# Moving a residual's transposes from TensorE to DMA, re-laying the last tokens' phases, and a new step order in a one-core attention and mixing kernel

## The chip, the core and the metric

The kernel runs on one core of one Trainium2 chip. The metric is the device time of one execution in microseconds (us). Runs more than 1.5% above the kernel's fastest count as slow and are left out of ratios. A ratio in this text is the mean time of one kernel's fast runs over the mean of the other's fast runs of the same rounds, so it is not quite the ratio of the medians that stand beside it. The 95% interval goes with it.

## The reference, cut to what matters

Inputs are q, k, v of 8 batches x 8 heads x 576 tokens x 64. The first half is attention twice: on tokens averaged by four (144 of them), repeated back, plus a band of seven tokens around each token. Its output becomes x, 576 tokens x 512 channels per batch. The second half is:

```python
theta = x @ w_theta
zr, zi = x * np.cos(theta), x * np.sin(theta)
y = w_tok_r @ zr + w_tok_i @ zi        # over tokens, per batch
u = x + y
return u + np.maximum(u @ w_ch, 0.0)
```

## The kernel before

One generator per step of a batch; a string of letters gives the order in which the steps are emitted, and every engine keeps exactly that order. L loads, C casts on POOL, A turns q and k, S scores, N and V attention outputs, T makes x transposed (channels on partitions), H phases, Z modulation, X mix, R channels, O output. PSUM has two wide slots and four of one bank each, taken in rotation.

Phases and modulation work on 128 tokens at a time; the last 64 tokens stand twice on the partitions, once for cosine and once for sine:

```python
for c in range(5):                                   # H
    n = OC[c]                                        # 128, 128, 128, 128, 64
    for dc in range(4):
        for lo in range(0, P, n):                    # twice for the last 64
            nc.tensor.matmul(out=th[lo:lo + n, :], lhsT=xT[:, dc, P*c:P*c + n], rhs=wth[:, dc, :], ...)
    # ... sine and cosine on ACT
for c in range(5):                                   # Z
    # ... nc.tensor.transpose of xT into psxt, then DVE: z = psxt * (cos, sin)
```

The mix yields u transposed (`uT`); the channel step multiplies it by `w_ch` and also turns it back on TensorE for the residual:

```python
nc.tensor.matmul(out=psr, lhsT=uT[:, dc, P*c:P*c + P], rhs=wch[:, dc, :], ...)      # R, four of these
nc.tensor.transpose(out=psx[:, P*dc:P*dc + P], in_=uT[:, dc, P*c:P*c + P], identity=ident)   # and four
nc.scalar.activation(out=rel, in_=psr, func=AF.Relu)
nc.vector.tensor_tensor(out=osb, in0=rel, in1=psx, op=ALU.add)                      # O, then the store
```

The softmax here doesn't subtract the row's maximum and nothing guards it: scores larger than these inputs give would overflow.

## Time and profile before

| | before |
|---|---|
| time, runs seen with the prediction | 277.8 us (274.64 to 278.04) |
| profiled span | 272.3 us |
| first mix matmul | 55.3 us |
| last matmul | 266.7 us |
| TensorE idle between the two | 0.1 us |

### The profile page before, as it was taken

The page shows a single profiled execution, that of the slowest core. Times are in us where ns is not written, and L with a number is a line of the kernel's source. Part 1 is how long each engine was busy: PE and PEld are TensorE (multiplying, and loading weights), DVE is VectorE, ACT ScalarE, POOL GpSimd, SP SyncE. Part 2 cuts the span into 40 slices and gives each one's busy share as a digit, 9 for nine tenths or more (in the row PEclk, how much of TensorE's full clock was granted, in tenths as well). Part 3 has the DMA queues.
Part 4 walks back from the last instruction along what each step waited for, and adds up shares of the span by engine and source line. Part 5 has one row for each costly group of instructions (what it writes and reads, how often), then busy time and mean ns, then how long its engine had stood idle before and what let it go on. Part 6 is the DMA issues. An engine that isn't in the chain of part 4 may idle for free.

```text
span 272.3 us, 7503 instructions
## 1 busy us (share of the span) xinstructions
PE 250.1 (92%) x2965; PEld 175.7 (65%) x2992; DVE 188.4 (69%) x423; ACT 183.3 (67%) x338; POOL 159.2 (58%) x187
## 2 busy tenths in 40 slices
PE   0486988999999999999999999999999999999991
PEld 0344654688558865787568865877668766766761
DVE  4958798778664885578656875667887676765542
ACT  2644279655887778877987789769887976543031
POOL 4236855999839974597729790998956526200000
PEclk9999599999999999999999999999999999999999
DMA  7999999999889895899449962984491002201223
GB/s 199 247 237 287 258 218 216 211 202 262 144 193 235 197 206 132 175 204 204 130 115 226 209 166 56 197 211 130 138 217 30 19 2 79 79 22 39 87 89 135
DMA packets 107858, 43.57 MB, mean 160 GB/s; under 512 B 97456, under 2 KB 101552, under 8 KB 107824
## 3 DMA queue, kind: packets, MB, share of 16 engines
q1 hardware_dynamic: 107824, 43.10, 71.2%
q8 instruction: 23, 0.38, 0.6%
q14 instruction: 11, 0.09, 0.1%
HBM read 33.65 MB, written 9.44 MB: 158 GB/s over the span
## 4 chain that ended last, share of the span: by engine, by line
PE 78%; DMA 11%; POOL 3%; DVE 2%; ACT 2%; issue 1%; SPq 0%; DVEq 0%; POOLq 0%
PE psu L583 26%; PE psth L541 11%; PE psr L602 10%; PE pstr L322 6%; DMA st_v<-in_v_dram 5%; PE psxt L562 4%; PE psS L414 4%; PE psloc L491 4%; DMA stw_th<-in_moe_w_theta_dram 4%; PE xTps L521 3%; PE psx L607 2%; DMA stw_tok<-in_moe_w_tok_i_dram 2%; PE psnd L453 2%; PE psr L615 1%; PE wps L262 1%
## 5 line engine op out<-in xcount | busy, mean ns | idle before, releaser
L583 PE MATMUL psu<-WT,z 128*128 128x288 bf16 x576 | 79.7, 286 | 0.0
L583 PEld LDWEIGHTS <-z 128*128 128x128 bf16 x576 | 53.3, 98 | 13.3
L435 POOL TENSOR_SCALAR_AFFINE_SELECT pm<-pm 128x1024 bf16<-128x1024 bf16 (+1 forms) x35 | 36.7, 1050 | 38.5 <-ACT pm L422 38.4
L587 DVE TENSOR_TENSOR uT<-psu,xT 128x288 bf16<-128x288 f32 x64 | 29.2, 457 | 25.9 <-PE psu L583 25.2
L422 ACT ACTIVATE pm<-psS 128x1024 bf16<-128x1024 f32 (+1 forms) x40 | 38.5, 983 | 11.6 <-PE psS L414 11.4
L541 PE MATMUL psth<-wth,xT 128*128 128x512 bf16 (+1 forms) x181 | 39.9, 381 | 0.8
L437 POOL TENSOR_SCALAR_AFFINE_SELECT pm<-pm 128x1024 bf16<-128x1024 bf16 (+1 forms) x35 | 36.8, 1051 | 2.4
L636 DVE TENSOR_TENSOR osb<-rel,psx 128x512 f32<-128x512 f32 (+1 forms) x40 | 25.2, 632 | 18.7 <-ACT rel L627 13.7
L627 ACT ACTIVATE rel<-psr 128x512 f32<-128x512 f32 (+1 forms) x40 | 22.2, 556 | 22.6 <-PE psr L602 15.3
L602 PE MATMUL psr<-wch,uT 128*128 128x512 bf16 x114 | 32.2, 380 | 0.7
L564 DVE TENSOR_TENSOR z<-psxt,cs 128x1024 bf16<-128x1024 bf16 (+1 forms) x40 | 24.6, 632 | 9.5 <-PE psxt L562 6.9
L500 DVE TENSOR_TENSOR tmp<-psloc,rl 120x512 bf16<-120x512 f32 (+1 forms) x40 | 27.6, 690 | 1.4
L547 ACT ACTIVATE cs<-psth,pihc 128x512 bf16<-128x512 f32 x32 | 22.1, 689 | 8.6 <-PE psth L541 7.9
L139 POOL CAST v_w<-st_v 128x1024 bf16<-128x1024 f32 (+1 forms) x24 | 21.0, 899 | 10.9 <-DMA st_v<-in_v_dram 10.9
L522 DVE TENSOR_TENSOR xT<-xTps,xdT 128x480 bf16<-128x480 bf16 (+1 forms) x40 | 24.8, 631 | 2.7 <-PE xTps L521 2.5
L325 ACT CAST kT<-pstr 128x384 bf16<-128x384 f32 x36 | 17.5, 485 | 8.3 <-PE pstr L322 8.1
L541 PEld LDWEIGHTS <-xT 128*128 128x128 bf16 (+1 forms) x192 | 14.0, 101 | 13.1 <-issue 3.3
L325 ACT CAST qT<-pstr 128x384 bf16<-128x384 f32 x36 | 16.2, 483 | 9.1 <-PE pstr L322 8.9
L133 POOL CAST k_tm<-st_k 96x1024 bf16<-96x1024 f32 x18 | 18.5, 1037 | 4.7 <-DMA st_k<-in_k_dram 4.7
L548 ACT ACTIVATE cs<-psth 128x512 bf16<-128x512 f32 x32 | 19.0, 592 | 0.0
L491 PE MATMUL psloc<-v_w,pm 128*128 128x65 bf16 (+1 forms) x320 | 17.0, 197 | 2.1 <-DVE xd L466 1.8
L133 POOL CAST q_tm<-st_q 96x1024 bf16<-96x1024 f32 x18 | 18.3, 1037 | 0.0
(98 smaller groups left out, 423.0 us busy)
## 6 DMA issues: line engine op xcount, KB each, us to landing
st_v<-in_v_dram SPq DMA_DIRECT2D x32, 256.0 KB, 5.4
out_dram<-osb SPq DMA_DIRECT2D x32, 256.0 KB, 2.4
st_q<-in_q_dram SPq DMA_DIRECT2D x36, 192.0 KB, 4.5
st_k<-in_k_dram SPq DMA_DIRECT2D x36, 192.0 KB, 4.6
st_q<-in_q_dram SPq DMA_DIRECT2D x8, 288.0 KB, 5.7
st_k<-in_k_dram SPq DMA_DIRECT2D x8, 288.0 KB, 5.3
st_v<-in_v_dram SPq DMA_DIRECT2D x8, 200.0 KB
stw_tok<-in_moe_w_tok_r_dram SPq DMA_DIRECT2D x4, 288.0 KB, 4.8
```

The source lines that it names most:

```text
L133: eng[i](out=dst[:, 2 * c:2 * c + 2].rearrange("p c h d -> p (c h d)"), in_=staged.pop((b, f"{'qk'[i]}{c}"))[0:TR])
L325: nc.scalar.copy(out=To[:, :, TR * c:TR * c + TR], in_=ps[:, :, 0:TR])
L422: nc.scalar.activation(out=pv, in_=ps[0:kw].rearrange("p e (j w) -> p (e j) w", w=P)[:, :, 0:qn], func=AF.Exp, scale=SCL,)
L435: nc.gpsimd.affine_select(out=pv, in_=pv, compare_op=ALU.is_ge, fill=0.0, base=off, pattern=[[0, 8], [-1, qn]], channel_multiplier=1)
L437: nc.gpsimd.affine_select(out=pv, in_=pv, compare_op=ALU.is_ge, fill=0.0, base=6 - off, pattern=[[0, 8], [1, qn]], channel_multiplier=-1)
L491: nc.tensor.matmul(out=pv[0:qn, par, j, :], lhsT=pms[b][c][0:kw, 4 * par + j, 0:qn], rhs=v_w[0:kw, c, 2 * j + par, 0:65], start=(j == 0), ...
L500: nc.vector.tensor_tensor(out=tmp[0:cnt].rearrange("p (j e d) -> p e j d", e=2, j=4), in0=pv[0:cnt, :, :, 0:D], in1=rl[0:cnt].unsqueeze(3) ...
L541: nc.tensor.matmul(out=th[lo:lo + n, :], lhsT=xT[:, dc, P * c:P * c + n], rhs=wth[:, dc, :], start=(dc == 0), stop=(dc == 3),)
L583: nc.tensor.matmul(out=ps[:, 0:288], lhsT=z[:, j, P * dc:P * dc + P], rhs=WT[:, j, cols], start=(j == 0), stop=(j == 8),)
L587: nc.vector.tensor_tensor(out=uT[:, dc, cols], in0=ps[:, 0:288], in1=xT[:, dc, cols], op=ALU.add)
L602: nc.tensor.matmul(out=psr, lhsT=uT[:, dc, P * c:P * c + P], rhs=wch[:, dc, :], start=(dc == 0), stop=(dc == 3),)
L636: nc.vector.tensor_tensor(out=osb[:, 0:w], in0=rel[:, 0:w], in1=psx[:, 0:w], op=ALU.add)
```

## The change

Its intent: take work from TensorE, the bound.

1. Residual: `uT` is turned by DMA transposes (SBUF to SBUF) issued by SyncE, and one DVE operation does relu and addition.

```diff
-nc.tensor.transpose(out=psx[...], in_=uT[:, dc, P*c:P*c + P], identity=ident)
-nc.scalar.activation(out=rel, in_=psr, func=AF.Relu)
-nc.vector.tensor_tensor(out=osb, in0=rel, in1=psx, op=ALU.add)
+# in the mix, as soon as a chunk of 128 channels is complete
+nc.sync.dma_start_transpose(out=ur[:, :, P*dc:P*dc + P], in_=uT[:, dc, 0:512])
+nc.gpsimd.tensor_copy(out=ut[:, dc % 2, HALF*(dc // 2):...], in_=uT[:, dc, 512:576])
+if dc >= 2: nc.sync.dma_start_transpose(out=utr[:, dc - 2, :].unsqueeze(1), in_=ut[:, dc - 2, :])
+# in the output
+nc.vector.scalar_tensor_tensor(out=osb, in0=psr, scalar=0.0, in1=ur[:, c, :], op0=ALU.max, op1=ALU.add)
```

2. Phases of the last 64 tokens: computed with channels on partitions, multiplied there, and turned by one DMA transpose. Their modulation step disappears.

```diff
+for ec in range(4):
+    for dc in range(4):
+        nc.tensor.matmul(out=th[:, ec, :], lhsT=wth[:, dc, P*ec:P*ec + P], rhs=xT[:, dc, 512:576], ...)
+# ... two sines of 256, zT = xT * (cos, sin)
+nc.sync.dma_start_transpose(out=z[:, 8, :].rearrange(...), in_=zT.rearrange(...))
```

3. q and k of batches 0 and 1 are loaded as nine tokens a partition on 128 partitions (before: six on 96), and the casts of batch 0 move from DVE and ACT to ACT and POOL. 4. A new order string for the whole program, and four output tiles for two.

More of the change, by code (lines that the diff above doesn't have):

```diff
@@ L35 @@
 WIDE = 2
+WR = 9
+WP = S // WR
 TR = 96
-NTR = 6
 TP = TR // 4
@@ L92, in load @@
                     nc.sync.dma_start(
-                        out=stage(b, f"{nm}{hh}")[0:TR, 0:2 * NTR * D].rearrange("p (h e) -> p h e", h=2),
-                        in_=src[b, 2 * hh:2 * hh + 2].rearrange("h (p r) d -> p h (r d)", r=NTR),
+                        out=stage(b, f"{nm}{hh}")[:, 0:WR * D],
+                        in_=src[b, 2 * hh:2 * hh + 2].rearrange("h (p r) d -> (h p) (r d)", r=WR),
                     )
@@ L116, in cast @@
     def cast(b):
-        q_tm = work.tile([TR, NTR, H, D], BF16, tag="q_tm", bufs=1, name=f"q_tm{b}")
-        k_tm = work.tile([TR, NTR, H, D], BF16, tag="k_tm", bufs=1, name=f"k_tm{b}")
+        dims = [P, 2, WR, 2, D] if b < WIDE else [P, 6, H, D]
+        q_tm = work.tile(dims, BF16, tag="q_tm", bufs=1, name=f"q_tm{b}")
+        k_tm = work.tile(dims, BF16, tag="k_tm", bufs=1, name=f"k_tm{b}")
         v_w = v_ws[b % 2]
@@ L125, in cast @@
                 for i, dst in enumerate((q_tm, k_tm)):
-                    eng[i](out=dst[:, :, 2 * hh:2 * hh + 2, :].rearrange("p r h d -> p h r d"),
-                           in_=staged.pop((b, f"{'qk'[i]}{hh}"))[0:TR, 0:2 * NTR * D].rearrange(
-                               "p (h r d) -> p h r d", h=2, d=D))
+                    eng[i](out=dst[:, hh // 2, :, hh % 2, :],
+                           in_=staged.pop((b, f"{'qk'[i]}{hh}"))[:, 0:WR * D].rearrange("p (r d) -> p r d", d=D))
                     yield
@@ L132, in cast @@
                 for c in range(3):
-                    eng[i](out=dst[:, 2 * c:2 * c + 2].rearrange("p c h d -> p (c h d)"),
+                    eng[i](out=dst[0:TR, 2 * c:2 * c + 2].rearrange("p c h d -> p (c h d)"),
                            in_=staged.pop((b, f"{'qk'[i]}{c}"))[0:TR])
@@ L158 @@
     nc.vector.tensor_copy(out=ip[:, 0:TR], in_=ident[0:TR, 0:TR])
-    pihc = const.tile([P, 2], FP32, name="pihc")
+    pihc = const.tile([P, 1], FP32, name="pihc")
     nc.vector.memset(pihc, PIH)
-    nc.vector.memset(pihc[HALF:P, 1:2], 0.0)
     kdPs = []
@@ L216 @@
     dve, act, gp = nc.vector.tensor_copy, nc.scalar.copy, nc.gpsimd.tensor_copy
-    CASTS = {0: (dve, act, gp), None: (gp, gp, gp)}
+    CASTS = {0: (act, gp, gp), None: (gp, gp, gp)}
     wth = wpool.tile([P, 4, DM], BF16, name="wth")
@@ L292, in turns, with wide_turn @@
         parts[b] = (qT, kT, qdT, kdP)
-        def wide_turn(n, hh):
+        def wide_turn(n, i):
             tm, To = ((q_tm, qT), (k_tm, kT))[n]
-            ps = w2(f"pstr{n}{hh}_{b}")
-            for r in range(NTR):
-                nc.tensor.matmul(
-                    out=ps[:, r // 3, (r % 3) * TR:(r % 3) * TR + TR],
-                    lhsT=tm[:, r, 2 * hh:2 * hh + 2, :], rhs=ip[:, 0:TR], start=True, stop=True,
-                )
-            (dve if n == 1 else act)(
-                out=To[:, hh, :].rearrange("p (w k c) -> p w k c", k=2, c=3),
-                in_=ps[:, :, 0:3 * TR].rearrange("p k (c w) -> p w k c", w=TR),
-            )
+            pss = [w2(f"pstr{n}{2 * i + a}_{b}") for a in range(2)]
+            for r in range(WR):
+                for a in range(2):
+                    nc.tensor.matmul(
+                        out=pss[a].rearrange("p k e -> p (k e)")[:, WP * r:WP * r + WP],
+                        lhsT=tm[WP * a:WP * a + WP, i, r, :, :], rhs=ident[WP * a:WP * a + WP, WP * a:WP * a + WP],
+                        start=True, stop=True,
+                    )
+            for a in range(2):
+                hh = 2 * i + a
+                (dve if n == 1 and a == 1 else act)(
+                    out=To[:, hh, :].rearrange("p (w r) -> p w r", r=WR),
+                    in_=pss[a].rearrange("p k e -> p (k e)")[:, 0:S].rearrange("p (r w) -> p w r", w=WP),
+                )
@@ L307, in wide_turn @@
             with nc.allow_low_precision(reason="sums are taken in float32 and rounded once"):
+                hs = slice(2 * i, 2 * i + 2)
                 if n == 0:
-                    nc.vector.tensor_reduce(out=qdT[:, hh, :], in_=To[:, hh, :].rearrange("p (m j) -> p m j", j=4),
-                           axis=AX.X, op=ALU.add)
-                else:
-                    nc.vector.tensor_reduce(out=kdP[:, hh, 0:4, 0:30],
-                       in_=To[:, hh, 0:480].rearrange("p (g m j) -> p g m j", g=4, j=4),
-                           axis=AX.X, op=ALU.add)
-                    nc.vector.tensor_reduce(out=kdP[:, hh, 4, 0:24], in_=To[:, hh, 480:576].rearrange("p (m j) -> p m j", j=4),
-                           axis=AX.X, op=ALU.add)
+                    nc.vector.tensor_reduce(out=qdT[:, hs, :], in_=To[:, hs, :].rearrange("p e (m j) -> p e m j", j=4),
+                                            axis=AX.X, op=ALU.add)
+                else:
+                    for hh in range(2 * i, 2 * i + 2):
+                        nc.vector.tensor_reduce(out=kdP[:, hh, 0:4, 0:30],
+                                                in_=To[:, hh, 0:480].rearrange("p (g m j) -> p g m j", g=4, j=4),
+                                                axis=AX.X, op=ALU.add)
+                    nc.vector.tensor_reduce(out=kdP[:, hs, 4, 0:24],
+                                            in_=To[:, hs, 480:576].rearrange("p e (m j) -> p e m j", j=4),
+                                            axis=AX.X, op=ALU.add)
@@ L322, in turn @@
                 nc.tensor.matmul(
-                    out=ps[:, hh, :], lhsT=tm[:, c, 2 * hh:2 * hh + 2, :], rhs=ip, start=True, stop=True,
+                    out=ps[:, hh, :], lhsT=tm[0:TR, c, 2 * hh:2 * hh + 2, :], rhs=ip, start=True, stop=True,
                 )
@@ L334, in turn @@
                                    in_=ps[:, :, TR + lo - TP * c:TR + hi - TP * c])
-        for i in range(8 if b < WIDE else 12):
+        for i in range(4 if b < WIDE else 12):
             if b < WIDE:
@@ L363, with slot @@
     pds, pms, xds, tmps = {}, {}, {}, {}
+    def slot(b, h):
+        return (2 * (h // 4) + h % 2, h // 2 % 2) if b < WIDE else (h // 2, h % 2)
     def scores(b):
@@ L394, in scores @@
         for h in range(H):
-            par, r = h % 2, KP * (h % 4)
+            r = KP * (h % 4)
+            blk, par = slot(b, h)
             nc.tensor.matmul(
                 out=ps[r:r + KP, h // 4, SD:2 * SD],
-                lhsT=kdP[64 * par:64 * par + 64, h // 2, 4, :],
-                rhs=qdT[64 * par:64 * par + 64, h // 2, :],
+                lhsT=kdP[64 * par:64 * par + 64, blk, 4, :],
+                rhs=qdT[64 * par:64 * par + 64, blk, :],
                 start=True, stop=True,
@@ L452, in pooled_out @@
             for h in range(H):
+                blk, par = slot(b, h)
                 nc.tensor.matmul(
                     out=pv[:, h // 4, h % 4, :],
-                    lhsT=pd[:, h, QD * g:QD * g + QD], rhs=vd[:, 0, h, 0:65],
+                    lhsT=pd[:, 2 * blk + par, QD * g:QD * g + QD], rhs=vd[:, 0, h, 0:65],
                     start=(h % 4 == 0), stop=False,
@@ L488, in outputs @@
             pv = ps[:, :, 0:260].rearrange("p e (j w) -> p e j w", w=65)
-            for par in range(2):
-                for j in range(4):
-                    nc.tensor.matmul(
-                        out=pv[0:qn, par, j, :],
-                        lhsT=pms[b][c][0:kw, 4 * par + j, 0:qn],
-                        rhs=v_w[0:kw, c, 2 * j + par, 0:65],
-                        start=(j == 0), stop=(j == 3),
-                    )
+            for h in range(H):
+                blk, par = slot(b, h)
+                nc.tensor.matmul(
+                    out=pv[0:qn, h // 4, h % 4, :],
+                    lhsT=pms[b][c][0:kw, 4 * par + blk, 0:qn],
+                    rhs=v_w[0:kw, c, h, 0:65],
+                    start=(h % 4 == 0), stop=(h % 4 == 3),
+                )
             rl = work.tile([P, 2, 4], FP32, tag="rl", name=f"rl{c}_{b}")
@@ L500, in outputs @@
             nc.vector.tensor_tensor(
-                out=tmp[0:cnt].rearrange("p (j e d) -> p e j d", e=2, j=4),
+                out=tmp[0:cnt].rearrange("p (e j d) -> p e j d", e=2, j=4),
                 in0=pv[0:cnt, :, :, 0:D],
@@ L535, in phases @@
         xT = xTs[b]
-        for c in range(5):
+        z = zs[b] = moep.tile([P, 9, DM], BF16, tag="z", name=f"z{b}")
+        for c in range(4):
             th = w1(f"psth{c}_{b}")
-            n = OC[c]
             for dc in range(4):
-                for lo in range(0, P, n):
-                    nc.tensor.matmul(
-                        out=th[lo:lo + n, :], lhsT=xT[:, dc, P * c:P * c + n], rhs=wth[:, dc, :],
-                        start=(dc == 0), stop=(dc == 3),
-                    )
-            cs = css[b, c] = moep.tile([P, 2, DM], BF16, tag="cs", bufs=3, name=f"cs{c}_{b}")
-            if c < 4:
-                nc.scalar.activation(out=cs[:, 0, :], in_=th, func=AF.Sin, bias=pihc[:, 0:1], scale=1.0)
-                nc.scalar.activation(out=cs[:, 1, :], in_=th, func=AF.Sin, bias=0.0, scale=1.0)
-            else:
-                nc.scalar.activation(out=cs[:, 0, :], in_=th, func=AF.Sin, bias=pihc[:, 1:2], scale=1.0)
-            yield
+                nc.tensor.matmul(
+                    out=th, lhsT=xT[:, dc, P * c:P * c + P], rhs=wth[:, dc, :],
+                    start=(dc == 0), stop=(dc == 3),
+                )
+            cs = css[b, c] = moep.tile([P, 2, DM], BF16, tag="cs", bufs=3, name=f"cs{c}_{b}")
+            nc.scalar.activation(out=cs[:, 0, :], in_=th, func=AF.Sin, bias=pihc, scale=1.0)
+            nc.scalar.activation(out=cs[:, 1, :], in_=th, func=AF.Sin, bias=0.0, scale=1.0)
+            yield
@@ new lines, in phases @@
+        th = w1(f"pstt_{b}")[:, 0:4 * HALF].rearrange("p (e t) -> p e t", e=4)
+        for ec in range(4):
+            for dc in range(4):
+                nc.tensor.matmul(
+                    out=th[:, ec, :], lhsT=wth[:, dc, P * ec:P * ec + P], rhs=xT[:, dc, 512:576],
+                    start=(dc == 0), stop=(dc == 3),
+                )
+        cst = moep.tile([P, 4, 2, HALF], BF16, tag="cst", bufs=1, name=f"cst_{b}")
+        nc.scalar.activation(out=cst[:, :, 0, :], in_=th, func=AF.Sin, bias=pihc, scale=1.0)
@@ L553, in modulate @@
+        nc.scalar.activation(out=cst[:, :, 1, :], in_=th, func=AF.Sin, bias=0.0, scale=1.0)
+        zT = moep.tile([P, 4, 2, HALF], BF16, tag="zT", bufs=1, name=f"zT_{b}")
+        nc.vector.tensor_tensor(
+            out=zT, in0=xT[:, :, 512:576].unsqueeze(2).to_broadcast([P, 4, 2, HALF]), in1=cst, op=ALU.mult,
+        )
+        nc.sync.dma_start_transpose(
+            out=z[:, 8, :].rearrange("p (e d) -> p e d", e=4), in_=zT.rearrange("p e r t -> p (e r t)"),
+        )
+        yield
     def modulate(b):
-        xT = xTs[b]
@@ L556, in modulate @@
-        z = zs[b] = moep.tile([P, 9, DM], BF16, tag="z", name=f"z{b}")
-        for c in range(5):
+        xT, z = xTs[b], zs[b]
+        for c in range(4):
             ps = w1(f"psxt{c}_{b}", BF16)[:, 0:DM]
-            n = OC[c]
             for dc in range(4):
-                for lo in range(0, P, n):
-                    nc.tensor.transpose(out=ps[lo:lo + n, P * dc:P * dc + P], in_=xT[:, dc, P * c:P * c + n], identity=ident)
-            m = 2 if c < 4 else 1
+                nc.tensor.transpose(out=ps[:, P * dc:P * dc + P], in_=xT[:, dc, P * c:P * c + P], identity=ident)
@@ L564, in modulate @@
             nc.vector.tensor_tensor(
-                out=z[:, 2 * c:2 * c + m, :], in0=ps.unsqueeze(1).to_broadcast([P, m, DM]),
-                in1=css.pop((b, c))[:, 0:m, :],
-                op=ALU.mult,
+                out=z[:, 2 * c:2 * c + 2, :], in0=ps.unsqueeze(1).to_broadcast([P, 2, DM]),
+                in1=css.pop((b, c)), op=ALU.mult,
             )
             yield
-    uTs = {}
+    uTs, urs = {}, {}
     def mix(b):
@@ L577, in mix @@
         uT = uTs[b] = moep.tile([P, 4, S], BF16, tag="uT", name=f"uT{b}")
+        ur = moep.tile([P, 4, DM], BF16, tag="ur", name=f"ur{b}")
+        ut = moep.tile([P, 2, P], BF16, tag="ut", bufs=1, name=f"ut{b}")
+        utr = moep.tile([P, 2, P], BF16, tag="utr", name=f"utr{b}")
+        urs[b] = ur, utr
         for dc in range(4):
@@ L587, in mix @@
                 nc.vector.tensor_tensor(out=uT[:, dc, cols], in0=ps[:, 0:288], in1=xT[:, dc, cols], op=ALU.add)
+                if hf == 1:
+                    nc.sync.dma_start_transpose(out=ur[:, :, P * dc:P * dc + P], in_=uT[:, dc, 0:512])
+                    nc.gpsimd.tensor_copy(out=ut[:, dc % 2, HALF * (dc // 2):HALF * (dc // 2) + HALF], in_=uT[:, dc, 512:576])
+                    if dc >= 2:
+                        nc.sync.dma_start_transpose(out=utr[:, dc - 2, :].unsqueeze(1), in_=ut[:, dc - 2, :])
                 yield
@@ L596, in channels @@
         for c in range(5):
-            psr = w1(f"psr{c}_{b}")
-            psx = w1(f"psx{c}_{b}", BF16)
+            psr = rels[b, c] = w1(f"psr{c}_{b}")
             if c < 4:
-                w = DM
                 for dc in range(4):
@@ L605, in channels @@
                     )
-                for dc in range(4):
-                    nc.tensor.transpose(
-                        out=psx[:, P * dc:P * dc + P], in_=uT[:, dc, P * c:P * c + P], identity=ident,
-                    )
             else:
-                w = DM // 2
                 for dc in range(4):
@@ L615, in channels @@
                         nc.tensor.matmul(
-                            out=psr[64 * hf:64 * hf + 64, 0:w], lhsT=uT[:, dc, 512:576],
-                            rhs=wch[:, dc, w * hf:w * hf + w],
+                            out=psr[64 * hf:64 * hf + 64, 0:256], lhsT=uT[:, dc, 512:576],
+                            rhs=wch[:, dc, 256 * hf:256 * hf + 256],
                             start=(dc == 0), stop=(dc == 3),
                         )
-                for j in range(2):
-                    for hf in range(2):
-                        nc.tensor.transpose(
-                            out=psx[64 * hf:64 * hf + 64, P * j:P * j + P],
-                            in_=uT[:, 2 * hf + j, 512:576], identity=ident,
-                        )
-            rel = moep.tile([P, DM], FP32, tag="rel", name=f"rel{c}_{b}")
-            nc.scalar.activation(out=rel[:, 0:w], in_=psr[:, 0:w], func=AF.Relu)
-            rels[b, c] = (rel, psx, w)
             yield
     def store(b):
+        ur, utr = urs.pop(b)
         for c in range(5):
-            rel, psx, w = rels.pop((b, c))
-            osb = moep.tile([P, DM], FP32, tag="osb", name=f"osb{c}_{b}")
-            nc.vector.tensor_tensor(out=osb[:, 0:w], in0=rel[:, 0:w], in1=psx[:, 0:w], op=ALU.add)
+            psr = rels.pop((b, c))
+            w = DM if c < 4 else DM // 2
+            osb = moep.tile([P, DM], FP32, tag="osb", bufs=4, name=f"osb{c}_{b}")
+            nc.vector.scalar_tensor_tensor(
+                out=osb[:, 0:w], in0=psr[:, 0:w], scalar=0.0,
+                in1=ur[:, c, :] if c < 4 else utr.rearrange("p j d -> p (j d)"), op0=ALU.max, op1=ALU.add,
+            )
             if c < 4:
@@ L642, in store @@
             yield
-    FIRST = (
-        "LCLACLLCAALCCLALLCALCACLAASCLDSCLSCSLAlDVSLNNLcVVCLlNClcATDALTSClCADTCSlVccLlllCcLcCCHlVLTcclHTCLcLA"
-        "ZlcZClLAHAAHHLLDCSAccAWLCZSLSWCCWWSWWCCLWSCLWWSZZLNASAAlXLVClXAXLAVAAXcANAXNTVAXcATLXSCVTAHCVXTHLTZH"
-        "CRHOCZLCHLZSZZRROCOSXARLCLLROLLO"
-    )
-    PERIOD = (
-        "SSXAXAANCAXAASCNAXACNLVLAXCLAVVALAXTSSCTTRROCOVACHLVXTHTZHZHHZROCSZLLZRCLLOSRXO"
-    )
-    PERIODS = 3
-    LAST = (
-        "LASLNAAXAACSXCALANAACCVXCAXSSCNXVAAXCAVAAROSSTTRSOCSXTAALVRSROTSVHONLTHVLZNHZLHZHZZACVCASNXXTAVAXAAC"
-        "LCVXAVARCTSSOXATSSTXTHNXVHZZHNVHHNZSXZRZORSSOXTTVRROVHOXXXTROVXTXZTHHZHXXZZHZRORROXOXXRXOXXXROROXROR"
-        "ROORO"
+    ORDER = (
+        "LLLCCCLCLLDLlLALCLlALCClLACCClALcScSSlCSSCAcVlLclCCSDVNNlcVLcLcDLCCVLNTTSlclTCALlHVLCTCcZLCLHAlDTLAH"
+        "cCAHLCcLLHcSWCWZLAWCLSSZWAWNSCWLWWCCSZAWALLNXLSACVNXTAASXVAAAXXLACTVLXlClAVXVAXCSCSTLTACSDAATSHNcHNZ"
+        "HNCcVHZVLHLCTZSLZCARSOTRLOCACARSLLALAOCXAROVXCAAXVAROALHVTCXSSXXCATASSZXALTCHHXVNHNAHAVCSNALRLLSLLCT"
+        "LORROOCAAZLSZZATCVRCOXALXALXTXAVVXCLASCXSASTSACXTHNHVNZHAVCCHZXACNROATAHTLSZZSRLORLOLRSRLHLOOCLVAXXC"
+        "ACVATAAVXTATCHHZXHXAZCHALLCSCZXSXAZSSXLNCARLASLLCONXAAVSXNVXCLSCAAAXATVRAOXVRAOAXTSRCTCSORSVOXACLSTS"
+        "RTHNOXNAVZHVZCHLHNHLLRSZLCRLLLRCOOCOTCZRSAOXAAXATXAAAVVXAAXCTATAVCCSXSTSROXASSHXVHNNHZHNZVHTZSRORTSO"
+        "ZROVXHTVXXTVHZHXTXZHZHXZROXRXOXXXXROXXROXXRORORRRORROOROOO"
     )
@@ L685 @@
     pin()
-    for s in FIRST + PERIOD * PERIODS + LAST:
+    for s in ORDER:
         next(sequences[s])
```

## The prediction

> **What bounds the kernel now.** I read the page first (busy shares, slices), then the chain that ended last in order of time, then four windows cut at the landmarks of that chain, then the groups by form, the DMA issues, and SyncE's own waits. The windows carry most of the argument. Columns: length, then busy us and instructions of PE, PEld, DVE, ACT and POOL, the granted clock, the DMA engines' mean busy share, GB/s.
>
> ```profile
> 0.00:47.00 47.00, 31.93 (x324) 19.27 (x328) 36.15 (x96) 25.02 (x36) 24.54 (x45) 0.93 1.05 238
> 47.00:55.50 8.50, 8.30 (x139) 5.96 (x137) 6.64 (x16) 5.67 (x9) 7.89 (x10) 1.00 1.24 210
> 55.50:204.00 148.50, 147.56 (x1848) 106.22 (x1862) 104.59 (x232) 118.22 (x234) 110.95 (x116) 1.00 0.83 179
> 204.00:272.30 68.30, 62.35 (x661) 44.30 (x666) 40.97 (x82) 34.36 (x63) 15.84 (x17) 1.00 0.18 59
> ```
>
> Three stages. To 47 us the DMA engines are full (share 1.05 at 238 GB/s) and PE isn't. From 55.5 us, where the first mix matmul of batch 0 stands, PE is busy 147.6 of 148.5 us, and it stays so to its last matmul at 266.7. The third stage is a tail of 5.6 us. The chain shows what ends the first stage, the start of the second, and the tail:
>
> ```profile
> 17.92 9.70 DMA stw_th<-in_moe_w_theta_dram
> 33.48 7.37 DMA st_v<-in_v_dram
> 41.09 6.39 DMA stw_tok<-in_moe_w_tok_i_dram
> 47.54 1.29 POOL wtm L248 x2
> 48.87 1.12 PE wps L262 x11
> ...
> 55.47 1.10 PE psu L583 x9
> ...
> 265.46 0.70 DVE osb L636
> 266.18 2.00 DMA out_dram<-osb
> 268.30 0.42 DVE osb L636
> ```
>
> The start waits for the last token weight (landed 47.5), is then cast and turned by PE, and only then can a mix run. At the end the chain runs PE, relu, addition, store; the last addition waits for a store to free one of only two output tiles.
>
> **What PE pays for the parts that go.** These pieces of the chain, in order of time, are PE's issue spacing, which is what counts where PE never idles (the busy column overlaps matmuls and overstates it):
>
> ```profile
> 56.57 0.24 PE psloc L491 x8
> ...
> 137.09 0.22 PE psx L607 x4
> ...
> 139.91 0.56 PE psr L615 x8
> 140.47 0.11 PE psx L622 x4
> ...
> 246.50 0.98 PE psth L541 x8
> 247.48 0.22 PE psxt L562 x8
> ```
>
> Four 128x128 transposes of the residual cost 0.22 us, the last 64 tokens' four 0.11. The eight phase matmuls of those tokens cost 0.98, not eight times the 0.215 of a full 512-column one: their two halves of the array run together. Their eight transposes cost 0.22. The first row is there for its shape: eight matmuls of 65 columns on 128 rows of weights take 0.24.
>
> **What the Trainium skill says.** (1) "DMA: Bandwidth & Descriptors", section "Latency and other measured facts": an X-bar transpose ran at 261 GB/s with a non-contiguous middle dimension. No DMA transpose is in this trace, so this is the size I use, and it is the weakest number here. (2) Same page, "Anatomy of one DMA": about 2.0 us fixed, mostly the write's receipt. That is for another issuing path, but this trace agrees: with the DMA engines nearly idle after 204 us, a 64 KB store landed in 1.9 us and a 256 KB one in 2.0. (3) Same page, "Queues, rings and completion order": each DMA engine takes descriptors in ring order, so a transpose issued by SyncE stands behind the loads issued before it. The trace agrees in so far as stores landed in 4.2 us at 111 to 141 us, beside loads, against 2.0 without them. (4) "VectorE: DVE Perf Modes", "The perf-mode tier table": an operand in PSUM with fp32 keeps an element-wise operation at the slow rate. The trace agrees: additions and products reading a 512-wide fp32 tile take 0.69 us. So the joined relu and addition should cost what the addition alone does.
>
> **Part by part, for one batch.**
>
> Residual by DMA: PE loses 16 + 4 transposes = 4 x 0.22 + 0.11 = 0.99 us. ACT loses five relus (40 take 22.2 us: 2.8 us per batch), which lay beside PE. DVE keeps its five additions at 0.69 and 0.42; their inputs change to a PSUM tile and bf16 from SBUF. POOL gains four small copies, some 0.25 us each as an estimate from the 0.26 us that a 128x96 cast takes on DVE, so about 1 us on an engine at 58%. SyncE gains four transposes of 128 KB and two of 32 KB.
>
> Last tokens' phases transposed: PE loses 0.98 + 0.22 = 1.20 and gains 16 matmuls of 64 columns. Taking psloc's spacing for nearly the same shape, these cost 0.48. ACT does two sines of 256 instead of one of 512 (0.69 to about 2 x 0.39, going by the 256-wide relu). DVE trades one 512-wide product for another. SyncE gains one transpose of 128 KB.
>
> Sum on PE: 0.99 + 1.20 - 0.48 = 1.71 us per batch, 13.7 us for eight. About 1 us of it belongs to batch 0's phases before 55.5 us, where PE waits anyway: 12.7 on the path.
>
> Nine tokens a partition: q, k of batches 0 and 1. 96 matmuls of 96 columns become 144 of 64 with half the rows; by the trace's 0.11 us (cold) to 0.055 per old one and about 0.034 for half-row matmuls (16 scores in 0.55 us) this is near 5 us both times, all before or about the first mix. POOL casts batch 0's k, too, four casts near 0.67 us, while it has idle time waiting for loads. Nothing here moves the end.
>
> New order: I priced each step of both order strings with the chain's spacings. From the first mix step to the end PE has 206.0 us of steps before and 194.4 after: 11.6 less, near the 12.7 above, the rest being which steps stand before the first mix. The real stretch is 211.2 us (55.5 to 266.7), a factor of 1.025. After: 199.3. The start does not move in my count: in both orders the last token weight is the byte at 10.7 MB of the sequence of loads, and the same bytes stand in front of it. Since PE has no idle time left after 55.5 us, the order alone can win nothing there; it can only keep the gain.
>
> The tail: the last mix is now followed by nine channel steps and 6.3 us of PE work, meant to hide the transposes. Four output tiles instead of two take away the wait of 1.1 us at the end. I take 4.7 us instead of 5.6.
>
> Undisturbed: 55.5 + 199.3 + 4.7 = 259.5 us of profile against 272.3, a ratio of 0.953; on the median of 277.8, 264.7.
>
> **Rivals.**
>
> DMA becomes a second bound. Per batch the transposes move 5 x 131 + 2 x 33 KB = 0.72 MB, at 261 GB/s 2.8 us (estimate from the skill's figure). Loads are out at 204 us before; in the new order at about 191. The loads and stores of that stage took 0.83 x 148.5 = 123 us of the DMA engines; in 136 us that is 0.91, and with five batches' transposes (14 us) 1.01. The engines have shown 1.05 over 47 us, so it just fits, with no slack. Against it: after that point they were at 0.18, so only loads can be late. If transposes are twice as slow, 1.11 and some 8 us of PE waits: 267 us of profile, time near 273.
>
> SyncE's queue becomes one. It issued for 20 to 23 us of each 29.2 us period (24 to 26 issues). Seven more at 0.36 us, its shortest store issue, add 2.5; at 1 us, as loads under pressure, 7, in a period of about 27.5. It issues in order, so a transpose waiting for its tile also holds the loads behind it. For it as a danger: SyncE waited 76 us for output tiles before and can do so harmlessly only while loads are ahead.
>
> The PE waits come back as waits for transposes. The first mix of a batch needs the transposed phases, six to twelve us of PE work later in the new order; the output needs the residual, as little as 4.3 us after the last mix step for one batch, and holds one of four PSUM tiles meanwhile. A transpose of about 2.5 us alone and 4 to 5 behind loads, after 0.46 us of addition, fits mostly. I allow 1 us in some batches.
>
> ACT or DVE being relieved gives the gain: against it PE's 99%.
>
> **Range and chances.** From 264.7 I add about 1.5 for waits on transposes or late loads: 266. Low end 256: start and tail each some us better and no waits. High end 279: transposes at a third of the assumed speed, or loads held by SyncE. Faster by over 2% means below 272.2: 0.68. Within 2%: 0.20. Slower: 0.12, for a transpose much slower than the skill says.
>
> **What would show it.** Right: first mix near 55 us; the residual's transposes gone from PE; PE busy 98% or more from 56 us on; transposes landing in 2 to 5 us; loads ending near 191. The joined operation should take 0.69 us. Wrong: long PE idle before mix or DVE idle before the outputs, released by a transpose; POOL idle before casts, released by loads, in mid-kernel; SyncE issuing without a pause; a DMA share at or above 1.0 all the way to 200 us.

## More of the kernel before

The page of the kernel before: busy time and share of each engine, then what the DMA queues moved and how large a part of the time their 16 engines worked on it.

```profile
PE 250.1 (92%) x2965; PEld 175.7 (65%) x2992; DVE 188.4 (69%) x423; ACT 183.3 (67%) x338; POOL 159.2 (58%) x187
...
DMA packets 107858, 43.57 MB, mean 160 GB/s; under 512 B 97456, under 2 KB 101552, under 8 KB 107824
...
q1 hardware_dynamic: 107824, 43.10, 71.2%
```

## The result, and the profile after

| | before | after |
|---|---|---|
| time, median | 276.42 us (274.64 to 278.04, 4 runs) | 267.42 us (266.81 to 272.88, 4 runs) |
| ratio | 1 | 0.968 (0.9589 to 0.977) |
| profiled span | 272.3 us | 266.2 us |
| first mix matmul | 55.3 | 51.2 |
| last matmul | 266.7 | 259.4 |
| TensorE idle between | 0.1 | 5.4 |
| after the last matmul | 5.5 | 6.8 |

All four runs before count as fast. But the kernel's runs beside the experiments fall into 272.68 to 276.23 us and 278.85 to 281.11 us, and two of these four (277.8 and 278.04) lie near the second group. Against the other two alone the ratio is 267.21 / 274.84 = 0.972, so the gain is better read as 2.8 to 3.2%.

The page of the changed kernel, the same lines as above, and the joined operation's row (busy us and mean ns, then idle of its engine before it):

```profile
PE 239.5 (90%) x2880; PEld 164.6 (62%) x2880; DVE 180.8 (68%) x406; ACT 165.9 (62%) x312; POOL 167.9 (63%) x223
...
DMA packets 131155, 49.34 MB, mean 185 GB/s; under 512 B 121777, under 2 KB 122801, under 8 KB 131121
...
q1 hardware_dynamic: 131120, 48.88, 84.2%
...
L654 DVE SCALAR_TENSOR_TENSOR osb<-psr,ur 128x512 f32<-128x512 f32 x32 | 21.5, 684 | 6.4 <-PE psr L632 4.3
```

The rows before that this one replaces, from the view of the kernel before that keeps shapes apart:

```profile
L636 DVE TENSOR_TENSOR osb<-rel,psx 128x512 f32<-128x512 f32 x32 | 22.0, 686 | 17.6 <-ACT rel L627 13.0 <-PE psSd L396 2.2 <-DMA st_k<-in_k_dram 1.3
L627 ACT ACTIVATE rel<-psr 128x512 f32<-128x512 f32 x32 | 19.1, 597 | 15.3 <-PE psr L602 15.3
```

PE is down 10.6 us and ACT 17.4. The joined operation takes 684 ns, as the addition of the same shape did (686 ns before). The DMA engines carry 5.8 MB more, in packets of which nearly all new ones are under 512 B; their busy share times the span went from 194 to 224 us.

Windows of the changed kernel, cut at its own landmarks (columns as in the prediction):

```profile
0.00:47.00 47.00, 32.60 (x431) 19.28 (x432) 33.45 (x85) 28.24 (x43) 29.18 (x55) 1.00 1.02 263
47.00:51.20 4.20, 4.20 (x74) 3.15 (x72) 3.36 (x10) 3.24 (x6) 4.13 (x4) 1.00 0.97 196
51.20:200.00 148.80, 143.75 (x1774) 101.27 (x1772) 103.64 (x230) 108.24 (x215) 113.14 (x134) 1.00 0.94 184
200.00:259.40 59.40, 58.96 (x611) 40.92 (x610) 37.82 (x80) 26.20 (x50) 21.49 (x32) 1.00 0.51 123
259.40:266.20 6.80, 0.00 (x0) 0.00 (x0) 2.50 (x4) 0.00 (x0) 0.00 (x0) 0.77 0.63 216
```

The third row answers to 147.56 of 148.50 before: PE now has 5 us without work there, in pieces below 1 us, released by DVE, ACT or POOL. (The 0.9 us missing before is mostly matmul records that the trace lacks; rows of equal matmuls joined, as in the table, leave 0.1.) The DMA share in it rose from 0.83 to 0.94. The last row, the tail, holds only DVE additions and stores.

Where TensorE's time went, worked out from the trace by giving each stretch of time to the tile whose matmuls end in it: residual transposes -8.1 us, phases -7.4 and +3.9 for their new form, modulation transposes -2.7, together -14.3. All other steps together +2.6, of which the banded scores are +1.5. They cost more in the runs with the new order (13.8 us in that of the order with nine tokens) than in the old one (12.5); that they lie less well beside their neighbours there is the likely reason, not a shown one. Total busy time by this count 251.4 to 239.6 (the first a little above the page's, from rounded rows).

The DMA transposes, from the changed kernel's DMA view (count, then median us from issue to landing):

```profile
ur<-uT SPq DMA_TRANSPOSE x32, 3.2
utr<-ut SPq DMA_TRANSPOSE x16, 2.3
...
z<-zT SPq DMA_TRANSPOSE x8, 3.3
```

And SyncE's queue over 10 us of mid-kernel (start, length, instruction, count):

```profile
97.70 2.52 SPq L616 DMA_TRANSPOSE ur<-uT  x2
100.31 1.19 SPq L619 DMA_TRANSPOSE utr<-ut  x1
101.56 1.15 SPq L104 DMA_DIRECT2D st_k<-in_k_dram  x2
103.29 1.99 SPq L616 DMA_TRANSPOSE ur<-uT  x1
105.38 1.18 SPq L619 DMA_TRANSPOSE utr<-ut  x1
107.74 1.20 SPq L576 DMA_TRANSPOSE z<-zT  x1
109.00 2.31 SPq L104 DMA_DIRECT2D st_k<-in_k_dram  x4
```

A transpose holds the queue for 1.12 us at least and some 1.2 in the median, a load of k or q for 0.31 at least and 0.53 to 0.59 in the median. The lengths of all SyncE's rows between 82 and 200 us add up to 110.6 of 118 us, against 84.5 before (merged rows, so short gaps between equal issues are counted in; issue by issue it is 107.7 against 74.8). Pauses longer than 0.3 us between two issues add up to 2.2 us there, against 36.8 before. The queue is nearly full.

### The profile page after: what moved, and what is told of

It is laid out like the page before. It is cut to its first block, busy times and chain, and to the rows that moved or that the text cites. A ratio compares the mean times of both kernels' runs of the same rounds, so it can differ in the third digit from the quotient of the medians.

```text
span 266.2 us, 7362 instructions
## 1 busy us (share of the span) xinstructions
PE 239.5 (90%) x2880; PEld 164.6 (62%) x2880; DVE 180.8 (68%) x406; ACT 165.9 (62%) x312; POOL 167.9 (63%) x223
## 3 DMA queue, kind: packets, MB, share of 16 engines
q1 hardware_dynamic: 131120, 48.88, 84.2%
## 5 line engine op out<-in xcount | busy, mean ns | idle before, releaser
L449 POOL TENSOR_SCALAR_AFFINE_SELECT pm<-pm 128x1024 bf16<-128x1024 bf16 (+1 forms) x35 | 36.8, 1051 | 2.4
L553 PE MATMUL psth<-wth,xT 128*128 128x512 bf16 x128 | 32.4, 379 | 0.6 <-DVE xT L535 0.4
L632 PE MATMUL psr<-wch,uT 128*128 128x512 bf16 x128 | 31.4, 379 | 0.6 <-DVE xT L535 0.6
L140 POOL CAST v_w<-st_v 128x1024 bf16<-128x1024 f32 (+1 forms) x24 | 21.9, 916 | 15.2 <-DMA st_v<-in_v_dram 15.2
L654 DVE SCALAR_TENSOR_TENSOR osb<-psr,ur 128x512 f32<-128x512 f32 x32 | 21.5, 684 | 6.4 <-PE psr L632 4.3
L617 POOL COPY ut<-uT 128x64 bf16<-128x64 bf16 x32 | 7.3, 237 | 27.7 <-DVE uT L614 22.6
L134 POOL CAST k_tm<-st_k 96x1024 bf16<-96x1024 f32 x18 | 18.9, 1051 | 7.8 <-DMA st_k<-in_k_dram 5.5
L588 DVE TENSOR_TENSOR z<-psxt,cs 128x1024 bf16<-128x1024 bf16 x32 | 21.5, 682 | 3.1 <-PE psxt L587 3.0
L332 ACT CAST qT<-pstr 128x384 bf16<-128x384 f32 x36 | 16.9, 484 | 8.6 <-PE pstr L329 8.5
L334 DVE CAST qdT<-pstr 128x96 bf16<-128x96 f32 x36 | 9.1, 255 | 17.4 <-ACT qT L332 16.9
L632 PEld LDWEIGHTS <-uT 128*128 128x128 bf16 x128 | 11.5, 97 | 11.7 <-DVE xT L535 0.6
```

The source lines that it names most:

```text
L134: eng[i](out=dst[0:TR, 2 * c:2 * c + 2].rearrange("p c h d -> p (c h d)"), in_=staged.pop((b, f"{'qk'[i]}{c}"))[0:TR])
L332: nc.scalar.copy(out=To[:, :, TR * c:TR * c + TR], in_=ps[:, :, 0:TR])
L449: nc.gpsimd.affine_select(out=pv, in_=pv, compare_op=ALU.is_ge, fill=0.0, base=6 - off, pattern=[[0, 8], [1, qn]], channel_multiplier=-1)
L553: nc.tensor.matmul(out=th, lhsT=xT[:, dc, P * c:P * c + P], rhs=wth[:, dc, :], start=(dc == 0), stop=(dc == 3),)
L632: nc.tensor.matmul(out=psr, lhsT=uT[:, dc, P * c:P * c + P], rhs=wch[:, dc, :], start=(dc == 0), stop=(dc == 3),)
```

## The experiments

Theory 1 after the result: the gain is the TensorE steps removed; the order keeps it but brings waits of its own. Rival A: the order (with its earlier first mix) gains. Rival B: transposes give back much of the gain through SyncE's queue and the DMA engines. Rival C: the POOL copies do. The kernel before ran beside each group, at 274.66, 275.23 and 274.66 us; ratios are to it, and are what is compared. The changed kernel itself did not run again beside them, so a distance to its 0.968 carries the doubt about that figure: it is 0.4 points smaller if 0.972 is the right one. The first mix of kernels with the same start lies anywhere from 50.8 to 53.9 us in their single profiles, so spans are compared by their parts.

**The new order and nine tokens alone.** Both other parts go back to TensorE.

```diff
-<residual by DMA, joined relu and addition; last tokens' phases transposed>
+<the old forms; the old modulation of the last tokens inside its H step; five O letters moved forward>
```

> New order and nine tokens a partition alone: residual and last tokens' phases go back to TensorE (five of the outputs come up to a few steps earlier in the order, since each then holds a second PSUM tile). Theory 1 (the gain is the TensorE steps removed, the order only keeps it): TensorE gets back 8.1 + 6.2 us of steps and loses some 4 us of waits, so 274 to 278 us, the time before within 1%. Rival A (the new order, with the first mix 4 us earlier, is what gains): 266 to 270 us.

Measured: 280.36 us, ratio 1.0247 (1.0177 to 1.0318): slower than the kernel before. TensorE busy 252.2 us, idle after the first mix 6.5 us, with no transposing DMA in the program. Rival A falls: the order with the nine tokens loses 2.5%. Between this run and the changed kernel the ratio goes from 1.025 to 0.968, so the two TensorE parts are worth some 5.3 to 5.7% of the time before together. The time lay above my 274 to 278: I hadn't counted that the order's waits stay. Not all of the 6.5 us need be the order's: a channel step holds two PSUM tiles here and one in the changed kernel, and 1.4 us of the waits end with the relu, which the change removed.

**Residual undone.**

```diff
-nc.sync.dma_start_transpose(...), nc.gpsimd.tensor_copy(...), nc.vector.scalar_tensor_tensor(...)
+nc.tensor.transpose(...), nc.scalar.activation(..., func=AF.Relu), nc.vector.tensor_tensor(...)
```

> Residual transposed on TensorE again, relu on ACT again; phases, nine tokens and order as in the changed kernel. Theory 1: +8.1 us of TensorE steps, minus up to 4 us of waits that transposes cause: 271 to 275 us. Rival A: within 1% of 267. Rival B (transposes give back most of what they win, through the DMA engines and SyncE's queue): 267 to 270 us, with TensorE's idle time after the first mix falling from 5 to near 0.

Measured: 276.11 us, ratio 1.0071 (1.0012 to 1.0131). The residual part is worth 3.9 points of ratio, 0.968 to 1.007 (3.5 from 0.972). TensorE's busy time is 8.5 us up, as theory 1 has it; idle did not fall but rose to 7.4. The time is a little above the range I gave, because I had expected waits to go with the transposes.

**Last tokens' phases undone.**

```diff
-16 matmuls of 64 columns, two sines of 256, product with channels on partitions, DMA transpose
+8 matmuls of 512 columns on halves of the array, one sine, 8 transposes, product from PSUM
```

> Last 64 tokens' phases on TensorE in the old form again (within the same step of the order), everything else as changed. Theory 1: TensorE gets back 7.4 + 2.7 - 3.9 = 6.2 us, minus about 1 us of waits: 271 to 274 us. Rival A: within 1% of 267. Rival B: 267 to 269.

Measured: 269.83 us, ratio 0.9854 (0.9801 to 0.9906): worth 1.7 points (1.3 from 0.972); the fast times, from different groups, are 2.7 us apart. I had expected 4 to 7 us. On its own tiles TensorE does pay 5.2 us more, but all TensorE time rises by 3.8, idle falls by 1.5, to 3.9, and the tail is 0.8 shorter. So part of this gain is given back as waits; which of its pieces makes them I did not separate.

**The parts in the old order.**

```diff
-ORDER = <new>
+ORDER = <old, less 8 A and 8 Z steps that no longer exist; 5 X moved ahead of the O that needs them>
```

> All three parts in the old order, less the steps that no longer exist, and with five mix steps moved ahead of the outputs that now need them. Theory 1 in its strict form (the order is neutral as far as TensorE's waits go): 267 to 270 us. Theory 1 with the order needed to hide the transposes (my belief): outputs stand one or two steps behind their channel step there, too close for a transpose of 3 us, so DVE and with it TensorE wait 1 us or more per batch: 272 to 280 us. Rival A: near the time before, 276, or slower.

Measured: 317.07 us, ratio 1.1568 (1.1485 to 1.165), far beyond what I expected. TensorE idles 40.9 us after the first mix. The longest of these waits in its profile (us in total, times, longest):

```profile
DVE osb L654 <- DMA ur<-uT: 32.0, 7, 7.2
PEld L356 <- DVE osb L654: 23.8, 3, 8.2
PE psvb L356 <- DVE osb L654: 23.0, 3, 7.9
...
PEld L610 <- DMA z<-zT: 8.5, 3, 3.9
```

Read them as a chain: an output stands too close behind the mix, so DVE waits for the transpose; the channel result keeps its PSUM tile meanwhile, and TensorE's next step waits for that tile. In all, 32.0 us of TensorE's idle end with such an output and 7.6 with a late z. The run is longer for two more reasons: TensorE's own work after the first mix took 209.8 us against 202.7 in the changed kernel, at a mean granted clock of 0.91 against 1.00 there, and the start is late. The new order is thus needed: it is not the gain, but the room in which 3 us of latency disappear. (The late start is that of nine tokens in the old order, see below: first mix at 60.7 us.)

**No transposes at all**, a wrong result.

```diff
-three nc.sync.dma_start_transpose calls
+outputs and mix read constant tiles instead
```

> The changed kernel with all 56 DMA transposes taken out; the outputs and the mix read constant tiles instead, so the result is wrong on purpose, the work of all compute engines stays. Theory 1 as it now stands (TensorE's 5 us of idle after the first mix are the new order's own, since the run of the order alone had 6.5 without any transpose): within 2.5 us of the changed kernel, idle after the first mix 4 to 6 us, a shorter tail by 1 to 2 us. Rival B (DMA engines at 0.94 and a full SyncE queue make the loads late): 4 to 6 us faster, idle near 0.

Measured: 265.19 us, ratio 0.965 (0.955 to 0.9751), not apart from 0.968. TensorE's idle after the first mix is 4.3 us, against 5.4; the tail 4.2 against 6.8. Its mid-kernel (the changed kernel's row of the same stretch stands under "Large transposes doubled"):

```profile
82.00:200.00 118.00, 115.95 (x1409) 81.23 (x1408) 80.15 (x180) 87.86 (x173) 84.98 (x102) 1.00 0.76 159
```

So in mid-kernel all 56 transposes together cost about 1 us of TensorE time, and the rest of the idle is not theirs. Rival B falls for the changed kernel as it stands, except in the tail.

**No POOL copies**, the last tokens' residual wrong.

```diff
-nc.gpsimd.tensor_copy(out=ut[...], in_=uT[:, dc, 512:576])
+ut is a constant tile
```

> The changed kernel without the 32 POOL copies; the small transposes read a constant tile, so the last tokens' residual is wrong on purpose. Rival C (the copies make POOL wait for TensorE, 27.7 us of idle before them, and its casts and selects come late): 2 to 5 us faster, TensorE's idle after the first mix down by 2 us or more. Theory 1: within 1 us.

Measured: 267.09 us, ratio 0.972 (0.9659 to 0.9781). Idle 4.4 us, tail 6.7. Rival C falls; POOL's 27.7 us of idle ahead of the copies cost nothing on the path.

**Eight output tiles.**

```diff
-osb = moep.tile([P, DM], FP32, tag="osb", bufs=4, ...)
+osb = moep.tile([P, DM], FP32, tag="osb", bufs=8, ...)
```

> The changed kernel with eight output tiles in place of four. In its tail the last addition waited for a store, and an earlier one 1.6 us. Theory 1: the tail of 6.8 us shrinks by about 1.5 to 2 us, nothing else moves: 265 to 266 us. If stores bound the tail anyway: no change.

Measured: 268.24 us, ratio 0.9756 (0.9683 to 0.983): no gain shown. The tail went from 6.8 to 6.0 us only, less than the 1.5 to 2 us I had expected; the stores then stood behind one another and behind the last two transposes on SyncE.

**Stores issued by ACT.**

```diff
-nc.sync.dma_start(out=out[...], in_=osb...)
+nc.scalar.dma_start(out=out[...], in_=osb...)
```

> The changed kernel with the 48 stores issued by ACT in place of SyncE, whose queue shows almost no pause from 82 to 200 us. Rival B in its form of a full SyncE queue: 2 to 4 us faster. Theory 1: within 1 us in mid-kernel; slower by some us if ACT, which issues in order, waits for outputs.

Measured: 272.13 us, ratio 0.9888 (0.978 to 0.9996). The tail fell to 4.2 us, but idle after the first mix rose from 5.4 to 8.6. SyncE's pauses above 0.3 us between 82 and 200 us rose from 2.2 to 19.8 us, and this did not help. It is no clean test of the queue, though: ACT keeps the order of its instructions, and waited some 30 us in all ahead of these stores, most of it for the outputs.

**Nine tokens alone, old order.**

```diff
+loads, casts, turns and head slots of batches 0 and 1 as in the change; nothing else
```

> The kernel before with one part alone: q and k of the first two batches as nine tokens a partition (and the casts of batch 0 placed as in the change), in the old order less the eight turn steps that fall away. Theory 1: nothing on the path, within 1% of the time before. Rival A': the larger packets bring the first mix forward by the 4 us seen in the changed kernel, and the time falls by 3 to 4 us.

Measured: four runs at 279.54 to 286.13 us, median 284.83; only one counts as fast, so there is no interval. It is not faster. The profile (span 277.7, against 272.3) has its first mix at 58.6 us, 3.3 later than before, and a tail of 7.2 us, 1.7 longer. It shows why the start is late (TensorE's waits):

```profile
PE pstr L300 <- POOL band L213: 7.0, 1, 7.0
```

The first k casts now stand behind POOL's building of constants, which the old order put first. Theory 1's "within 1%" and Rival A' both missed; the part needs its order, too.

**Large transposes doubled.**

```diff
-nc.sync.dma_start_transpose(out=ur[...], in_=uT[:, dc, 0:512])
+for t in (dup, ur): nc.sync.dma_start_transpose(out=t[...], in_=uT[:, dc, 0:512])
```

> The changed kernel with each of the 32 large residual transposes issued twice, the first time into a tile that nobody reads. Taking all 56 out won 2.3 us, all of it in the tail. Hidden with slack (theory 1, plain): doubling costs under 2 us. Hidden but at the edge (SyncE's queue has almost no pause from 82 to 200 us, and each large transpose holds it 1.2 us): 32 x 1.2 = 38 us more of issuing do not fit, loads come late, and it costs 8 us or more.

Measured: 299.85 us, ratio 1.0895 (1.0793 to 1.0998), some 32 us above the changed kernel, while taking 56 out won next to nothing. Windows of mid-kernel, first the changed kernel, then this one:

```profile
82.00:200.00 118.00, 114.41 (x1391) 80.27 (x1390) 81.78 (x179) 86.20 (x171) 85.62 (x102) 1.00 0.92 185
```

```profile
82.00:200.00 118.00, 104.40 (x1211) 72.48 (x1209) 67.23 (x152) 73.36 (x151) 75.09 (x90) 0.95 0.91 175
```

Its waits for DMA, and two of TensorE's own:

```profile
POOL k_tm L134 <- DMA st_k<-in_k_dram: 22.6, 10, 6.2
...
DVE osb L656 <- DMA ur<-uT: 13.6, 5, 6.2
...
PE pstr L329 <- POOL k_tm L134: 6.1, 2, 3.7
PE psr L642 <- DVE osb L656: 5.9, 1, 5.9
```

The DMA engines did no more per time than in the changed kernel (share 0.91, 175 GB/s), though they have shown more elsewhere (1.05 over the first 47 us before), and a load of k landed 4.1 us after its issue (median, 82 to 200 us), as in the changed kernel. So what came late was the issue, and the engines are unlikely to be what ran full; no run changed their load without changing SyncE's. SyncE's rows fill 112.1 of 118 us, about as full as in the changed kernel (110.6), but with 36 transposes among 114 issues in place of 28 among 117, so with fewer loads and stores; and where the changed kernel's queue has 15.1 us of pauses above 0.3 us between 200 and 240 us, this one has 0.4. The 5.5 us that POOL waited for k in the changed kernel became 22.6. Each large transpose held SyncE for 1.2 us, 32 of them 38 us.

How that reached TensorE: of its 27 us of idle after the first mix, 13.2 end with an output (DVE, which waits for `ur`), 6.1 with a cast of k and 3.3 with a late z. So the late transposes themselves cost more than the late loads, of which my expectation spoke. And idle is 22 of the 31 us by which the stretch from first mix to last matmul grew; in the other 9 TensorE's own work took longer (211.9 against 202.7 us), at a granted clock of 0.95 against 1.00. The changed kernel stands just short of this edge.

**A padded version.** One transpose per chunk moves all 576 tokens and some padding; the POOL copies, the small transposes and the half stores go.

```diff
-uT [P, 4, 576]; ur [P, 4, 512]; ut, utr; osb bufs=4
+uT [P, 4, 640], 64 columns zeroed; ur [P, 5, 512]; osb bufs=8
+nc.sync.dma_start_transpose(out=ur[:, :, P*dc:P*dc + P], in_=uT[:, dc, :])
+the last addition in two halves of 64 partitions
```

> A version meant to be better: the mix tile is padded to 640 tokens, so one transpose a chunk moves all 576, the last 64 tokens land in a fifth block, and the 32 POOL copies, the 16 small transposes and 8 of the stores go; the last addition is done in two halves of 64 partitions; eight output tiles. Theory 1: mid-kernel unchanged, the tail about 1.5 to 2.5 us shorter since SyncE issues one transpose and one store less there: 264 to 266.5 us. If SyncE's queue is what costs: 262 to 264.

Measured: correct, 265.13 us, ratio 0.9671 (0.9609 to 0.9733). The tail is 4.1 us against 6.8, idle about the same at 5.0. SyncE has 18.9 us of pauses above 0.3 us between 82 and 200 us where the changed kernel has 2.2: the same work, further from the edge.

**The same with ACT issuing the last batch's stores.**

```diff
-nc.sync.dma_start(out=out[...], in_=osb...)
+(nc.scalar if b == B - 1 else nc.sync).dma_start(out=out[...], in_=osb...)
```

> The padded version with the stores of the last batch alone issued by ACT, which has nothing left to do there, so that they need not stand behind SyncE's transposes. Theory 1: another 1 to 1.5 us off the tail against the padded version, nothing in mid-kernel: 263 to 265.5 us, the tail at 4.2 us as in the run without transposes.

Measured: correct, 264.5 us, ratio 0.9661 (0.9617 to 0.9705); tail 4.2 us, so the second edit adds nothing to the first. SyncE's rows fill 99.8 of 118 us here, merged as above. Both versions have the tail that was aimed at; that either is faster than the changed kernel (0.968) is not shown, since the intervals overlap.

## Why the prediction was right, point by point

- **The size.** Predicted 266.0 us, range 256 to 279, faster as the likeliest; measured 267.42. As a ratio I had 0.958 of 277.8 and the runs gave 0.968 (or 0.972): the gain was two thirds to three quarters of the one predicted. The profiles, which the sum was made for, gave less than half: 6.1 us (272.3 to 266.2) of 12.8. They make it up as follows: TensorE's time 251.4 to 239.6, idle before the first mix 15.2 to 14.4, idle after it 0.1 to 5.4, tail 5.5 to 6.8. So the mechanism was right, TensorE's time is where the gain is, and the two terms for waits and tail were mis-sized.
- **Luck in the number.** A span of 272.3 goes with a time of some 274 us, since span and time differ by 1.7 us. I scaled the predicted span by 277.8 instead, a run near the slower group. That put some 3.5 us into the 266.0 and brought it nearer to 267.42.
- **TensorE's removed steps: right.** Predicted 13.7 us, measured 14.3 on the tiles concerned. Reading the chain's spacings rather than the busy column made this close. Undoing the residual gave back 8.5 us of TensorE time, against 8 x 0.99 = 7.9.
- **The stretch from first mix to last matmul: too short.** Predicted 199.3 us, measured 208.2. Of the 8.9 us, 5.4 are idle where I had "I allow 1 us in some batches", 1.5 us in all. They are mostly the order's waits, not the transposes': 4.3 us stay with only the transposes taken out, and the run without any transposing DMA and without the new parts has 6.5. My rival "waits for transposes" named the wrong cause for the right symptom. The other 3.5 are TensorE time: steps that cost more in their new neighbourhood (2.6 over the whole kernel), and an error in my count of which steps stand before the first mix.
- **The start: too late.** I held it at 55.5; it came at 51.2. The same 37 loads stand ahead of the last token weight in both orders, as counted, but they went out faster: that weight was issued at 36.5 us in place of 42.5, and its cast ended at 42.9 in place of 48.8. With nine tokens in the old order the cast ended at 46.7, with the new order and nine tokens at 43.1, so both had a part. The step that failed is from "the same bytes" to "the same time". It won less than it seems: TensorE's idle before the first mix fell by 0.8 us only, and most of the 4.1 us is work that now lies behind the first mix, in the stretch above. Some 2.5 us of it is also within the scatter of single profiles.
- **The tail: too short.** Predicted 4.7, measured 6.8. The term missed was SyncE's issue time: the last two transposes and then ten stores go out one after another, and additions waited for stores. Without transposes, and in the padded version, it is 4.1 to 4.2.
- **The joined operation at 0.69 us: right**, 684 ns. **Transposes landing in 2 to 5 us: right**, 2.2 to 5.2 for the 25 of 56 whose landing the trace has. **Loads ending near 191 us: wrong**, the last was issued at 205.6. **PE busy 98% from 56 us on: nearly**, 198.6 of 203.4 us, 97.6%.
- **The DMA rival: right in its statement, small in effect.** I put the share at 1.01 in mid-kernel; it was 0.94, and taking the transposes away changed the time by 0.3 points, inside the interval.
- **The SyncE rival: the real edge.** I gave a transpose 0.36 to 1 us of issue; it takes 1.2. The queue went from 84.5 to 110.6 of 118 us. "SyncE issuing without a pause", which I had named as a sign of being wrong, came true, and it does no harm as it is: taking the transposes out won 1 us of idle. Doubling the large ones cost 32 us.
- **The order "can only keep the gain": right**, and stronger than put: with the nine tokens alone it loses 2.5%, and in the old one the parts lose 15.7% (some of it by the late start of the nine tokens and the lower clock).

What stays open: how the earlier start divides between order and nine tokens, how much of the loss in the two slowest runs is the granted clock, and which TensorE waits in the new order could be had back by another one.

## What to carry to other kernels

Where TensorE is busy without a gap, price a removed step by the spacing of its pieces in the chain in order of time, not by its busy sum, and expect the sum of those spacings as the gain in TensorE time (13.7 us priced, 14.3 measured); waits that a new order brings come off it (5.3 us here). Here a DMA transpose was a good exchange for TensorE steps where the order left the 2.2 to 5.2 us of its landing between producer and reader, and the issuing queue had 1.2 us free for each; check both, because the same parts gained 3% in one order and lost 16% in another. When a change is hidden, double it: taking the transposes away showed next to nothing, and doubling them showed how near the edge the kernel stands. Check a base, too, for two groups of times before scaling by it.

## What the Trainium skill lacked or had wrong

- "DMA: Bandwidth & Descriptors", section "Latency and other measured facts", gives 261 GB/s for a transpose with a non-contiguous middle dimension. Here 56 of them, 5.77 MB, took 84.2% of 266.2 less 72.6% of 264.6 (the run without them), 32 us of the DMA engines' time, 180 GB/s; the 32 doubled ones, 4.19 MB, took 83.7% of 297.4 less 84.2% of 266.2, 24.8 us, 169 GB/s. (Busy shares of 16 engines, so a rough figure.) The trace's packets of 256 B took 22 ns on average with the transposes and 23 without them, so per packet the transposes were no slower than the loads.
- The same page's section "DMA Transpose (X-bar)" doesn't say how long a transpose from SBUF to SBUF holds its issuing queue on this chip (the cycle counts that the page sets beside trn3's are for other sizes). Here it was 1.19 us at least and 1.20 in the median for 128 KB of phases, 1.12 and 1.18 for 32 KB: nearly the same for both sizes, and two to four times a plain store's 0.33 us at least and 0.53 in the median.
- "Advanced Engine Details and Errata", section "X-Bar Transpose (TRN2)", calls transposing DMAs as fast as regular ones. By landing that is so here only roughly (in the median 3.2 to 3.3 us for 128 KB and 2.3 for 32 KB, against 3.2 for a store of 256 KB and 2.1 for one of 64 KB in the same run); by time on the issuing queue it is not, as above.
